# Zeroed dummy products in the planned gaps of TensorE, in a talking-heads attention and squared-ReLU kernel

## The chip, the cores and the metric

The kernel runs on one core of one Trainium2 chip. The metric is the device time of one execution in microseconds (us); lower is better. The kernel before took 604.01, 604.84 and 604.93 us in three runs, a median of 604.84 us.

## What is computed

The reference, cut to what matters (8 batches, 12 heads, 448 rows, head size 64; 3584 rows of 768 in the feed-forward part, hidden size 2048):

```python
scores = (1 / sqrt(64)) * q @ k.T                      # per batch and head, 448 x 448
scores = einsum('bhij,hg->bgij', scores, w_pre)        # heads are mixed
attn = softmax(scores, axis=-1)
attn = einsum('bhij,hg->bgij', attn, w_post)           # heads are mixed again
x = (attn @ v) as rows of 768
out = square(relu(x @ w_in)) @ w_out
```

## The kernel before

**Stages.** A batch has four blocks of score rows: a tail block (r = 0) and three blocks of 128 rows (r = 1 to 3). `score` makes the scores of a block per pair of heads on TensorE (L465 for the tail, L470 for the pairs), and VectorE or ScalarE copies them from a PSUM bank to the tile `snat`, of which there are two (`copy`, L300 and L302). `relayout` (the transfers L498, issued by SyncE) moves them to `sch`, so that ten query rows with all twelve heads lie on 120 partitions: a chunk. A batch has 45 chunks. `chunk` takes each through these steps: `f_m`, a product with `wmix` that mixes the heads (L563); `f_max`, the row's extreme on VectorE (L568); `f_exp`, the exponential and its sum on ScalarE (L571); `f_rc`, the reciprocal on VectorE (L577); `f_wq`, the second mixing matrix scaled by it on GpSimd (L580); `f_at`, four products that mix and turn at once (L587); and `f_ac`, a copy to `atb`. When half of a batch's rows are there, `av` multiplies by `v` (L623, 48 products for one half) and ScalarE copies the result to `xt`. The feed-forward part works on units of 128 or 256 rows: L668 (hidden layer), ScalarE's ReLU (L681), GpSimd's square (L684), L700 (output), a VectorE copy, a store.

**The start.** Batch 0 and 1 turn q and k by TensorE (L353, for the tail rows L381); later batches by DMA. GpSimd issues the loads of q, k and v, and in batch 0 those of both weight matrices of the feed-forward part (L775 issues `w_in`); each of the weight loads is placed behind an `f_wq`.

**What sets the order.** Nothing of it is left to the scheduler of the framework. Every step is an `Op` with a planned duration, a priority, what it depends on, and the PSUM bank that it takes or gives back. `Planner.run` goes through the time of a plan: whenever an engine is free in the plan it takes the ready step with the lowest priority number, and the order in which the steps were taken is the order in which the kernel then issues them (`manual_schedule`). The planned durations are constants in the code (190 ns for `f_m`, 212 ns for `f_at`); the chip doesn't see them, only the order. Each engine runs its instructions strictly in the order issued, and each waits for what it needs. The eight PSUM banks are given out by the planner from the front of the list `free`. TensorE's steps have a mode (whole array, half of its rows, half of its columns), and the planner puts 95 ns on a change of mode (`TURN`). The products of the feed-forward part have priorities above 1e6 and so fill what attention leaves free; there is none before the first half of batch 0 is through `av`.

## Time and profile before

| what | value |
|---|---|
| median of three runs | 604.84 us |
| profiled execution, whole | 606.62 us |
| its span, first to last instruction | 604.8 us |
| TensorE (PE) busy | 571.2 us, 94% |
| VectorE (DVE) busy | 489.7 us, 81% |
| ScalarE (ACT) busy | 468.4 us, 77% |
| GpSimd (POOL) busy | 325.6 us, 54% |
| granted TensorE clock, mean | 0.968 |

The profile is of one execution. Its parts that are used below: the span cut in 40 slices of about 15 us, in which each digit is the busy share in tenths and PEclk is the clock that TensorE was granted, in tenths of full speed; the chain of work that ended last, followed back from the last instruction, with the time at which each piece began and its length; windows, with the busy time of each engine in a stretch (in brackets the number of instructions), the granted clock, the busy share of the DMA engines and the GB/s; the timeline of one engine, where square brackets give the idle time before a piece and what ended it. A line L465 is line 465 of the kernel before. The ends of matmuls are modelled in the profile, so that small gaps on PE are shown smaller than they are.

### The profile page before, as it was taken

To read this page: it belongs to the slowest core of one execution; us is meant where nothing else is said; L and a number is where in the kernel's file an instruction comes from. 1 tells how busy PE (TensorE), PEld (TensorE's weight loads), DVE (VectorE), ACT (ScalarE), POOL (GpSimd) and SP (SyncE) were. 2 spreads that over 40 slices of the span, in tenths; PEclk is the share of its full clock that TensorE was granted. 3 is DMA by queue.
4 is the path that set the end of the run, shared out by engine and by line. 5 is a ranking of instruction groups with operands and counts; after the bars stand their busy time and mean duration, and the time that the engine had idled before them with its cause. 6 is when DMAs were issued, how large, how long until landed. Compare 5 with 4: busy or idle time off the path is not lost.

```text
span 604.8 us, 16567 instructions
## 1 busy us (share of the span) xinstructions
PE 571.2 (94%) x5517; PEld 405.6 (67%) x5517; DVE 489.7 (81%) x1237; ACT 468.4 (77%) x1223; POOL 325.6 (54%) x595
## 2 busy tenths in 40 slices
PE   4678889999999999999999999999999999999996
PEld 2335646666767857675867867686777867687873
DVE  4777987879898998989799998999899989887011
ACT  2677888878889898898898878899888887985320
POOL 5353816733665727662774727672783644472530
PEclk9757999979999999999999999999999999999999
DMA  9799989974498539974597439964797426321011
GB/s 135 119 227 168 205 158 162 191 135 111 116 150 199 147 82 169 196 148 115 123 169 178 129 91 187 170 151 114 149 190 152 131 83 144 97 92 29 27 53 52
DMA packets 138222, 82.29 MB, mean 136 GB/s; under 512 B 59672, under 2 KB 134680, under 8 KB 138136
## 3 DMA queue, kind: packets, MB, share of 16 engines
q1 hardware_dynamic: 86744, 58.42, 37.9%
q0 software_dynamic: 51392, 22.81, 30.6%
q8 instruction: 43, 0.70, 0.5%
q14 instruction: 43, 0.35, 0.2%
HBM read 45.62 MB, written 11.01 MB: 94 GB/s over the span
## 4 chain that ended last, share of the span: by engine, by line
PE 86%; DVE 5%; DMA 5%; issue 2%; POOL 2%; ACT 1%; DVEq 0%; POOLq 0%; ACTq 0%
PE bank L700 24%; PE bank L668 23%; PE bank L587 13%; PE bank L563 11%; PE bank L623 7%; PE bank L470 6%; DMA sch<-snat 4%; PE bank L465 2%; DVE mn L568 2%; DVE snat L300 1%; DVE atb L300 1%; POOL wq L580 1%; DMA qt<-in_q_dram 1%; PE bank L353 0%; POOL w L775 0%
## 5 line engine op out<-in xcount | busy, mean ns | idle before, releaser
L571 ACT ACTIVATE es<-bank,mn 120x448 bf16<-120x448 f32 x360 | 229.5, 644 | 33.8 <-DVE mn L568 27.2
L580 POOL TENSOR_SCALAR wq<-wback,rc 120x120 bf16<-120x120 f32 x360 | 130.8, 367 | 211.9 <-DVE rc L577 128.9
L568 DVE TENSOR_REDUCE mn<-bank 120x1 f32<-120x448 f32 x360 | 211.0, 611 | 5.9 <-PE bank L563 5.1
L700 PE MATMUL bank<-w,h 128*128 128x384 bf16 x896 | 174.5, 326 | 0.1
L300 DVE CAST atb<-bank 112x480 bf16<-112x480 f32 (+3 forms) x235 | 142.9, 619 | 36.5 <-PE bank L587 33.4
L668 PE MATMUL bank<-xt,w 128*128 128x256 bf16 (+1 forms) x1536 | 163.8, 259 | 0.0
L587 PEld LDWEIGHTS <-es 120*112 120x112 bf16 (+1 forms) x1440 | 120.8, 134 | 46.2 <-issue 20.7
L668 PEld LDWEIGHTS <-w 128*128 128x128 bf16 x1536 | 133.2, 98 | 25.2 <-issue 5.0
L587 PE MATMUL bank<-wq,es 120*112 120x120 bf16 (+1 forms) x1440 | 132.2, 222 | 14.1 <-POOL wq L580 12.6
L684 POOL TENSOR_TENSOR h<-hr 128x512 bf16<-128x512 f32 x112 | 116.5, 1041 | 48.5 <-ACT hr L681 46.6
L700 PEld LDWEIGHTS <-h 128*128 128x128 bf16 x896 | 83.0, 97 | 55.3 <-issue 6.7
L563 PE MATMUL bank<-sch,wmix 120*128 120x448 bf16 x352 | 115.1, 365 | 3.6 <-DMA sch<-snat 3.1
L302 ACT CAST snat<-bank 128x448 bf16<-128x448 f32 x174 | 88.0, 540 | 19.3 <-PE bank L470 10.5
L300 DVE CAST snat<-bank 128x448 bf16<-128x448 f32 x162 | 96.1, 614 | 2.7 <-PE bank L470 1.8
L681 ACT ACTIVATE hr<-bank 128x512 f32<-128x512 f32 x112 | 67.1, 599 | 34.2 <-PE bank L668 29.0
L302 ACT CAST atb<-bank 112x480 bf16<-112x480 f32 (+2 forms) x149 | 78.7, 537 | 19.0 <-PE bank L587 17.6
L571 ACT ACTIVATION_READ_ACCUMULATOR es<-bank,mn 120x1 f32 x360 | 75.7, 210 | 0.0
L577 DVE RECIPROCAL rc<-sm 120x1 f32<-120x1 f32 x360 | 53.5, 154 | 18.6 <-ACT es L571 16.5
L715 DVE COPY osb<-bank 128x384 f32<-128x384 f32 x56 | 30.9, 552 | 39.5 <-PE bank L700 39.5
L470 PE MATMUL bank<-kt,qz 64*128 64x448 bf16 x288 | 50.9, 372 | 2.1 <-DVE qz L300 1.8
L563 PEld LDWEIGHTS <-wmix 120*128 120x128 bf16 x360 | 32.4, 99 | 21.3 <-issue 9.2
L623 PE MATMUL bank<-atb,vs 112*64 112x192 bf16 (+1 forms) x768 | 43.8, 275 | 0.0
(45 smaller groups left out, 228.0 us busy)
## 6 DMA issues: line engine op xcount, KB each, us to landing
sch<-snat SPq DMA_DIRECT2D x336, 105.0 KB
out_dram<-osb SPq DMA_DIRECT2D x23, 360.0 KB
vs<-in_v_dram POOLq DMA_DIRECT2D x16, 336.0 KB, 8.7
ks<-in_k_dram POOLq DMA_DIRECT2D x14, 336.0 KB, 9.0
qs<-in_q_dram POOLq DMA_DIRECT2D x14, 288.0 KB, 8.7
w<-in_moe_w_in_dram POOLq DMA_DIRECT2D x6, 512.0 KB, 20.0
w<-in_moe_w_out_dram POOLq DMA_DIRECT2D x4, 768.0 KB, 17.5
out_dram<-osb SPq DMA_DIRECT2D x8, 192.0 KB
```

The lines of the kernel that those rows point to most:

```text
L300: nc.vector.tensor_copy(out=out_, in_=in_)
L302: nc.scalar.copy(out=out_, in_=in_)
L470: nc.tensor.matmul(slot[:, 0:S], lhsT=qz[i][half, r - 1, at_, :], rhs=kt[i][half, :, at_, :], start=True, stop=True,)
L563: nc.tensor.matmul(slot[:, 0:S], lhsT=wm[0:rows, :], rhs=src[0:rows, :], start=True, stop=True,)
L568: nc.vector.tensor_reduce(out=mn[i][0:rows, :], in_=slots[mk][0:rows, 0:S], axis=AX.X, op=ALU.min)
L571: nc.scalar.activation(out=es[i][0:rows, 0:S], in_=slots[mk][0:rows, 0:S], func=ACT.Exp, scale=-1.0, bias=mn[i][0:rows, 0:1], accum_out=sm ...
L580: nc.gpsimd.tensor_scalar(out=wq[i][0:rows, :, 0:ns], in0=wback[0:rows, :, 0:ns], scalar1=rc[i][0:rows, 0:1], scalar2=1.0, op0=ALU.mult, o ...
L587: nc.tensor.matmul(slot[0:P_KEYS, jb * H * ns:(jb + 1) * H * ns], lhsT=es[i][0:rows, jb * P_KEYS:(jb + 1) * P_KEYS], rhs=wq[i][0:rows, :, ...
L623: nc.tensor.matmul(v_[64 * hh:64 * hh + 64, i, 0:nx], lhsT=vs[:, 2 * c2 + hh, jb, :], rhs=atb[half][:, jb, 2 * c2 + hh, :], start=(jb == 0 ...
L668: nc.tensor.matmul(slot[:, j * w:(j + 1) * w], lhsT=w1[c2][:, (f0 + j) * 128:(f0 + j + 1) * 128], rhs=xt[:, c2, a:z], start=(c2 == 0), sto ...
L684: nc.gpsimd.tensor_tensor(out=h2_[:, f0:f0 + nf, 0:w], in0=hr[gi % 2][:, :].rearrange("p (f c) -> p f c", f=nf), in1=hr[gi % 2][:, :].rear ...
L700: nc.tensor.matmul(slot[:, 0:384], lhsT=h2_[:, ft, mt * 128:(mt + 1) * 128], rhs=w2[:, ft, nt * 384:(nt + 1) * 384], start=(ft == 0), stop ...
```

## The change

A tile `still` of 128 x 256 zeros (bfloat16) is set by VectorE as its first instruction. `stand` is one matmul on it, 256 columns wide, into a PSUM bank that nobody owns at that moment; its result is never read. The planner issues one whenever TensorE is free in the plan, has no ready step, and a bank is free, up to 190000 ns of the plan; it counts 112 ns for it (224 ns before 6000 ns of the plan), in which TensorE takes nothing else. It uses the mode of the step before. Twelve more are issued ahead of everything else. Since planned steps now begin a little later where a dummy was put ahead of them, the order of the other steps changes as well.

```diff
+IDLE_NS, IDLE_COLS, IDLE_END = 112, 256, 190000
+IDLE_COLD, COLD_END = 224, 6000
...
+                if item is None and eng == "PE" and free and self.still and t < IDLE_END:
+                    op = Op({"PE": 0}, 0, 0, self.still, [], None, None, mode)
+                    op.eng, op.ns, op.at = "PE", IDLE_COLD if t < COLD_END else IDLE_NS, t
+                    order.append((op, [free[0], mode]))
+                    busy[eng] = t + op.ns
+                    heapq.heappush(events, (t + op.ns, n, None))
+                    n += 1
...
+    still = sb.tile([P, IDLE_COLS], BF16, name="still")
+    nc.vector.memset(still[:, :], 0.0)
...
+    def stand(slot, mode):
+        k_, m_ = P // 2 if mode == ROWS else P, P // 2 if mode == COLS else P
+        nc.tensor.matmul(
+            slot[0:m_, 0:IDLE_COLS], lhsT=still[0:k_, 0:m_], rhs=still[0:k_, :], start=True, stop=True,
+        )
+
+    pl.still = stand
...
+        for _ in range(12):
+            stand(banks[0], 0)
```

In the built program there are 382 of them, in 88 groups, where TensorE had 5517 matmuls before: 28 ahead of the first transpose (L381), 87 more up to the first `f_m`, 156 from there to the `f_at` behind the first `av`, 80 from there to chunk 59, 27 among the chunks 60 to 65 and 4 later. In every group the last dummy writes the bank that the next product takes; 62 of the 382 wait for the copy that frees it.

More of the change, by code (lines that the diff above doesn't have):

```diff
@@ L80, in __init__ @@
         self.banks, self.most = [], {}
+        self.still = None
     def add(self, eng, ns, pri, fn, deps=(), lat=60, bank=None, frees=None, mode=0):
@@ L185, in run @@
                         push(x)
-        assert len(order) == len(self.ops)
+        assert len(order) >= len(self.ops)
         return order
```

## The prediction, as it was put on record

> **What bounds the kernel now.** I read the slices first, then the chain of waits, then windows cut where the clock changes, then the timelines of PE and SP.

> ```profile
> PE   4678889999999999999999999999999999999996
> ...
> PEclk9757999979999999999999999999999999999999
> ```

> PE is at 9 tenths from the seventh slice (91 us) on: from there the end is PE's work, done without a gap. What is lost lies before, in idle time and in a clock of 5 to 7 tenths in slices 2 to 4 and 9. The windows give the edges.

> ```profile
> 23.40:47.30 23.90, 18.31 (x97) 9.37 (x96) 17.72 (x44) 16.79 (x47) 12.72 (x24) 0.50 1.25 199
> 50.70:57.50 6.80, 6.44 (x63) 5.16 (x63) 3.80 (x11) 5.17 (x16) 3.07 (x6) 0.50 1.02 164
> 57.50:88.00 30.50, 23.98 (x323) 17.55 (x323) 28.42 (x75) 26.20 (x71) 15.21 (x30) 1.00 1.11 186
> 88.00:116.00 28.00, 27.32 (x266) 19.68 (x264) 22.33 (x54) 22.80 (x59) 19.08 (x32) 1.00 0.96 170
> 116.00:122.40 6.40, 5.48 (x40) 2.66 (x39) 6.14 (x18) 6.13 (x17) 4.15 (x10) 1.00 0.73 197
> 122.40:129.20 6.80, 6.32 (x63) 5.37 (x63) 3.54 (x10) 4.73 (x12) 2.46 (x5) 0.50 0.70 129
> ```

> The first figure is the length, the second PE's busy time, the third from the end the clock. It is half in 23.4 to 47.3, 50.7 to 57.5 and 122.4 to 129.2 us. The start is half too, though no record says so: two products L465 take 0.91 us at 11.55 and 0.66 us at 13.49 (chain).

> But a slow PE costs only where the end waits for it. The chain in those stretches:

> ```profile
> 26.53 8.52 DMA sch<-snat
> ...
> 37.04 8.87 DMA sch<-snat
> ...
> 53.33 3.98 PE bank L623 x37
> ```

> ```profile
> 122.88 0.56 PE bank L587 x4
> 123.44 3.98 PE bank L623 x24
> 127.42 0.98 PE bank L587 x8
> 128.40 1.02 PE bank L563 x3
> ```

> From 26 to 46 us the chain is two relayout transfers of 8.5 and 8.9 us. The waits in the program's order name eight DMA counters in turn for them, so a ninth transfer waits for the first: the one of 26.53 landed at 35.05, and SP issued the eighth after it at 35.12. A faster PE does nothing there. From 51 to 57.8 and from 122.9 to 129.4 the chain is PE at half clock.

> **The change part by part.** *One dummy* is a product of 256 columns. The trace has that form: 12 of L668 in 1.31 us (chain, at 110.76), so 0.109 us at full clock and 0.22 at half. Its weight load lies beside the product before, as L668's do. The 382 take 41.6 us of PE at full clock. Each one placed where PE would wait anyway costs nothing; every other one costs 0.109 us.

> *The first 28*: the zeros are VectorE's first instruction, and VectorE begins at 0.90 us. 28 at half clock take 6.1 us and end near 7.2 us. PE's first real work begins at 7.84 us, when the tail of q lands: hidden. If that cover were short by a microsecond it would cost that microsecond.

> *The 87 up to the first `f_m`*: 9.5 us. Here the loads are early, and PE does not wait as the plan thinks:

> ```profile
> 7.84 0.80 PE L381 MATMUL bank<-ident,qt 128*128 128x128 bf16 x6 [7.84 <-DMA qt<-in_q_dram]
> 8.57 0.96 PE L353 MATMUL bank<-ident,ks 112*64 112x112 bf16 x16
> 9.64 0.90 PE L465 MATMUL bank<-kt,zt 128*128 128x448 bf16 x2
> ...
> 17.00 0.62 PE L470 MATMUL bank<-kt,qz 64*128 64x448 bf16 x4 [0.79 <-DVE qz L300]
> ```

> No wait stands before the transposes L353, while the changed order puts 13, 10, 10 and 11 dummies ahead of groups of them. PE's own work from 7.84 to 18.01 us is 8.6 us, of which 5.2 at half clock would be 2.6: 6.0 us. With 9.5 us of dummies the first `f_m` comes at 23.3 us, not 18.01: **5 us later**. What passes on is what the relayouts see. The first waits for the tails (49 of the 87 ahead of the last): 7.84 + 5.3 + 3.4 = 16.5 against 14.15 us, +2.4. The first of the next block waits for the last pairs (90 ahead, 9.8 us): +5, less 0.7 us in which SP was behind at that place (copies done at 20.68, issue at 21.37): about +4. Since the transfers are then held by their own eight places up to 49 us, this stays: +2.4 to +4.3; I take **+3.7**, near the latter, the one that the stream of eight begins with.

> *The 156 up to 57.8 us*: 17.0 us of dummies. PE's records in 18.0 to 57.5 us are 2.69 + 18.31 + 1.98 + 6.44 us busy; at full clock 2.69 + 9.16 + 1.98 + 3.22 = 17.0. Together 34 us in a stretch of 39.5: they fit, nearly without slack, so they cost nothing there as long as the clock is full. The gain: PE in the chain from 51.06 to 57.78 is 6.7 us (0.52, 0.49, 0.86, 0.40, 3.98, 0.47) at half clock; at full it is 3.35. So **-3.4**, and batch 0's `av` ends at +0.3.

> *The 80 up to 116 us*: 8.7 us, where PE's idle time is 6.5 + 0.7 = 7.2 us (first minus second figure of two windows above); gaps are shown too small, since the ends of matmuls are modelled. **+0.5**, between 0 and 1.5.

> *The 27 up to 122.4 us*: 2.9 us against 0.9 us idle by the records, but the chain from 116.9 to 122.8 us is VectorE and GpSimd, so that most of it is hidden: **+0.5**, between 0 and 2.0. They fill the gaps after which the clock falls. If it stays, the four pieces of chain above (6.54 us at half) take 3.27: **-3.3**.

> *Waits*: 62 dummies wait for the copy that frees their bank. In all 88 groups the next product takes the same bank and would wait for it. Nothing.

> *After 130 us* no dummy stands, but the order differs. PE is busy 59.92 of 60 us in 130 to 190; another order moves a dense stretch by changes of mode and small waits: between -1 and +1 us, taken as 0. The zeroing on VectorE (0.38 us for the larger one at 0.90 us) lies in idle time.

> Sum: +3.7 - 3.4 + 0.5 + 0.5 - 3.3 = -2.0 us. Against the profiled execution (span 604.8, whole 606.62 us) this is 604.6; the median of the runs, 604.84, stands 1.8 under that execution, so **602.8 us**.

> [...] In 118.9 to 122.4 us PE was busy 2.86 of 3.50 us, its longest wait was below 0.8 us, and yet the clock then halved; in 30.1 to 33.6 PE was dense and the clock did not rise. So busy time alone does not decide: 2.28 of 3.50 us busy at 71.1 to 74.6 kept the clock. [...]

> **The rivals.**
> 1. *The dummies are real work, slower.* The 107 behind 57.8 us take 11.7 us where the records show 8.1 idle. If the head's delay goes through whole (+5 - 3.4 = +1.6), PE then has no waits to fill, and the excess of 3.6 us is paid; with -3.3 for the clock at 122: 606.7 us. It decides from the point where PE waits less than 11.7 us between 57.8 and 122 us. For it: DVE is busy 28.42 of 30.50 us in 57.5 to 88, so PE's waits there belong to VectorE and are not lengthened; against it: the records show gaps too small.
> 2. *The clock at 122 falls all the same*, since gaps below a microsecond are not its cause: the sum without -3.3 is +1.3, 606.1 us, at the edge of 0.2%. For it: the kept clock at 71 us with more idle time; against it: no stretch at 95% or more lost the clock.
> 3. *Zeros don't count for the clock at all.* Then the dummies cost 0.22 us: 34 + 17 us in 18 to 57.5, some 12 us late, 616 us or more. For it: no row shows a product of zeros. Against it: nothing in the clock's edges follows data.
> 4. *The relayouts go faster*, since the first weight load comes later behind the first `f_wq` and the early transfers escape it: the head passes on 2.4 us or less, 601 us. I count it to the forecast.

> **How the numbers follow.** Forecast with 4: 0.57, of it 0.50 faster by over 0.2% and 0.07 within 0.2%; rival 1: 0.22, slower; rival 2: 0.16, of it 0.08 within 0.2%, 0.08 slower; rival 3: 0.05, slower. 0.2% is 1.2 us, about what a measurement of this kernel can tell from no change. So faster 0.50, same 0.15, slower 0.35. The forecast's own range is 600.5 to 604.9: its ends are -4.3 (head +2.4, both +0.5 at 0) and +0.1 (head +4.3, one +0.5 at 2.0). The reordering moves the lower end to 600.0, taken at half its size. For 8 in 10 the range reaches over rivals 1 and 2: 600.0 to 607.0.

> **What would show it.** Right: PEclk full from about 8 us to 130 us; the first `f_m` at 22 to 24 us; `av` (L623) of batch 0 taking 2 us, ending near 57.5 us; L623 at 122 us taking 2 us. Wrong: a first `f_m` near 18 us (the dummies at the head are hidden); dummies of 0.2 us; the relayout transfers no longer in the chain; or, in 58 to 122 us, PE dense and each chunk later than before.

## The result: slower by 0.28%, and the profile after

The changed kernel takes 606.64 us in the median of 9 runs, the kernel before 604.93 us in the median of 9 beside it: ratio 1.0028, 95% interval 1.0017 to 1.0038. One of the nine executions of the changed kernel took 674.77 us at a mean granted clock of 0.85; the ratio leaves it out. The forecast was 602.8 us; the sign was wrong. The profiled execution after has a span of 605.6 us, against 604.8. In every run of both kernels the time lies 1.8 us over the span. So the execution that I had before me (606.62 us) was itself 1.7 us longer than the kernel's median, which matters below.

The clock did what the change sets out to do. The slices of the page, after:

```profile
PE   8999899999999999999999999999999999999996
...
PEclk9999999999999999999999999999999999999999
```

And the windows that were shown of before (length, PE busy, then PEld, DVE, ACT, POOL, the clock, DMA share, GB/s):

```profile
23.40:47.30 23.90, 23.33 (x222) 16.74 (x218) 20.51 (x51) 17.59 (x47) 13.00 (x24) 1.00 1.02 169
50.70:57.50 6.80, 6.80 (x94) 5.17 (x95) 6.34 (x18) 6.49 (x19) 2.72 (x7) 1.00 1.01 177
57.50:88.00 30.50, 27.53 (x372) 21.16 (x366) 25.47 (x67) 24.93 (x67) 15.37 (x29) 1.00 1.14 185
88.00:116.00 28.00, 28.00 (x273) 20.12 (x271) 23.00 (x57) 21.90 (x58) 17.29 (x30) 1.00 0.97 167
116.00:122.40 6.40, 6.40 (x64) 4.80 (x62) 6.14 (x17) 5.79 (x16) 5.38 (x11) 1.00 0.76 221
122.40:129.20 6.80, 6.80 (x67) 4.53 (x67) 6.80 (x19) 6.39 (x20) 3.08 (x7) 1.00 0.79 148
```

The clock is whole from 6.3 to 603.6 us, and PE is never idle for long. Yet a busy PE is not a gain when what fills it is dummies. PE's timeline after (L861 is the dummy, L365 the transposes, L680 the hidden layer of the feed-forward part, L599 `f_at`):

```profile
8.41 1.58 PE L861 MATMUL bank<-still 128*128 128x256 bf16 x13
9.92 0.58 PE L365 MATMUL bank<-ident,ks 112*64 112x112 bf16 x16
...
11.48 1.25 PE L861 MATMUL bank<-still 128*128 128x256 bf16 x10
12.66 0.58 PE L365 MATMUL bank<-ident,ks 112*64 112x112 bf16 x16
```

```profile
63.97 1.24 PE L680 MATMUL bank<-xt,w 128*128 128x128 bf16 x19 [1.63 <-DMA w<-in_moe_w_in_dram]
73.01 0.37 PE L599 MATMUL bank<-wq,es 120*112 120x120 bf16 x4 [1.03 <-POOL wq L592]
```

A group of 16 transposes takes 0.58 us in place of 0.96, but 13 dummies of 0.109 us stand ahead of one group and 10 ahead of the next, where PE did not wait before. Later PE waits 1.63 us for the last piece of `w_in`, a wait that was not there before. It comes with the new order, as the experiments show: that order without any dummy has it too (1.31 us). Where the time went, from the starts of the same steps in both traces (us):

| step | before | after | difference |
|---|---|---|---|
| first `f_m` | 18.01 | 23.66 | +5.65 |
| first `av` of batch 0 begins | 53.26 | 55.60 | +2.34 |
| its last product ends | 57.31 | 57.77 | +0.46 |
| second `av` of batch 0 begins | 91.38 | 94.83 | +3.45 |
| first `av` of batch 1 begins | 123.37 | 128.73 | +5.36 |
| its last product ends | 127.42 | 130.90 | +3.48 |
| last `av` begins | 557.2 | 559.9 | +2.7 |

The steps stand in another order, so that the difference at one step is no difference in the work done; at the end it is the spans' 0.8 us.

### The profile page after: what moved, and what is told of

Same layout as the page of the kernel before. It is cut to its first block, busy times and chain, and to the rows that moved or that the text cites. A ratio compares the mean times of both kernels' runs of the same rounds, so it can differ in the third digit from the quotient of the medians.

```text
span 605.6 us, 17331 instructions
## 1 busy us (share of the span) xinstructions
PE 594.1 (98%) x5899; PEld 429.8 (71%) x5899; DVE 487.7 (81%) x1240; ACT 475.2 (78%) x1232; POOL 321.2 (53%) x584
## 4 chain that ended last, share of the span: by engine, by line
PE 91%; DMA 5%; POOL 2%; issue 1%; DVE 0%; ACT 0%; DVEq 0%; POOLq 0%; ACTq 0%
PE bank L680 24%; PE bank L712 24%; PE bank L599 13%; PE bank L575 11%; PE bank L635 6%; PE bank L482 6%; DMA w<-in_moe_w_in_dram 4%; PE bank L861 4%; PE bank L477 2%; PE bank L365 1%; DMA qt<-in_q_dram 1%; POOL wq L592 1%; POOL w L787 0%; POOL qt L255 0%; POOL ks L260 0%
## 5 line engine op out<-in xcount | busy, mean ns | idle before, releaser
L312 DVE CAST atb<-bank 112x480 bf16<-112x480 f32 (+2 forms) x226 | 136.2, 616 | 37.7 <-PE bank L599 34.5
L680 PE MATMUL bank<-xt,w 128*128 128x256 bf16 (+1 forms) x1536 | 163.7, 259 | 1.6 <-DMA w<-in_moe_w_in_dram 1.6
L680 PEld LDWEIGHTS <-w 128*128 128x128 bf16 x1536 | 132.8, 98 | 26.3 <-issue 5.5
L599 PEld LDWEIGHTS <-es 120*112 120x112 bf16 (+1 forms) x1440 | 115.4, 130 | 29.2 <-issue 8.4
L599 PE MATMUL bank<-wq,es 120*112 120x120 bf16 (+1 forms) x1440 | 126.8, 217 | 1.4 <-POOL wq L592 1.3
L575 PE MATMUL bank<-sch,wmix 120*128 120x448 bf16 x352 | 111.9, 354 | 0.6 <-DVE atb L312 0.6
L314 ACT CAST atb<-bank 112x480 bf16<-112x480 f32 (+2 forms) x158 | 83.5, 538 | 14.7 <-PE bank L599 13.0
L861 PE MATMUL bank<-still 128*128 128x256 bf16 (+1 forms) x382 | 58.7, 281 | 1.4 <-DVE still L266 1.1
L482 PE MATMUL bank<-kt,qz 64*128 64x448 bf16 x288 | 48.3, 357 | 0.0
L861 PEld LDWEIGHTS <-still 128*128 128x128 bf16 (+1 forms) x382 | 37.0, 100 | 11.8 <-DVE still L266 1.1
```

The lines of the kernel that those rows point to most:

```text
L312: nc.vector.tensor_copy(out=out_, in_=in_)
L314: nc.scalar.copy(out=out_, in_=in_)
L482: nc.tensor.matmul(slot[:, 0:S], lhsT=qz[i][half, r - 1, at_, :], rhs=kt[i][half, :, at_, :], start=True, stop=True,)
L575: nc.tensor.matmul(slot[:, 0:S], lhsT=wm[0:rows, :], rhs=src[0:rows, :], start=True, stop=True,)
L599: nc.tensor.matmul(slot[0:P_KEYS, jb * H * ns:(jb + 1) * H * ns], lhsT=es[i][0:rows, jb * P_KEYS:(jb + 1) * P_KEYS], rhs=wq[i][0:rows, :, ...
L680: nc.tensor.matmul(slot[:, j * w:(j + 1) * w], lhsT=w1[c2][:, (f0 + j) * 128:(f0 + j + 1) * 128], rhs=xt[:, c2, a:z], start=(c2 == 0), sto ...
```

## The experiments

In the kernels a, b and d the planner and so the order of all other steps are those of the changed kernel (b4 moves two loads), and only the issue of the dummies differs, by the time that the plan gives them; the kernels c keep the order of the kernel before. For a2_no_head the edit reads

```diff
+KEEP = ((0, 3500), (21900, 200000))
...
         for op, args in pl.run():
+            if op.fn is stand and not any(a <= op.at < z for a, z in KEEP):
+                continue
             op.fn(*args)
```

Main theory at the start: the head's dummies cost the time, by way of the late last load of `w_in`, and the order is neutral. Rivals: the order costs; or the 107 dummies behind 57.8 us do. Each ratio is to runs of the kernel before on the same chip (medians 604.82 to 605.16 us). The executions of one row spread over 1 to 7 us, so that a difference of about 1 us between two rows is not told from none.

| label | dummies issued | median us | ratio, 95% interval |
|---|---|---|---|
| a1_none | none | 602.56 | 0.9963, 0.9945 to 0.9981 |
| b7_open_28 | 28 opening | 600.78 | 0.9936, 0.9911 to 0.9960 |
| d3_156 | 28 + 156 | 600.72 | 0.9933, 0.9917 to 0.9950 |
| d2_156_half | 28 + 156 of half width | 601.84 | 0.9951, 0.9933 to 0.9969 |
| a2_no_head | 28 + 267 | 602.03 | 0.9950, 0.9934 to 0.9967 |
| b3_no_head_no_80 | 28 + 156 + 31 | 602.47 | 0.9948, 0.9928 to 0.9968 |
| a4_only_27 | 27 | 602.88 | 0.9947, 0.9928 to 0.9967 |
| d1_head_half | 28 + 87 of half width | 603.51 | 0.9984, 0.9963 to 1.0004 |
| b6_head_only | 28 + 87 | 607.85 | 1.0039, 1.0021 to 1.0057 |
| a3_no_80 | all but 80 | 607.40 | 1.0033, 1.0018 to 1.0048 |
| b4_w_in_early | all, two loads moved | 606.52 | 1.0020, 1.0004 to 1.0035 |
| c3_before_open_28 | before's order, 28 | 603.40 | 0.9982, 0.9970 to 0.9993 |
| c4_before_27 | before's order, 27 | 605.43 | 1.0005, 0.9995 to 1.0015 |

**The order alone** (KEEP empty, and not the first 12).

> The changed kernel's own order of all other steps, but none of the 382 dummies is issued. It gives the price of the new order alone. Main theory (the new order is about neutral; the loss comes from the dummies at the head, which delay the last load of w_in, and nothing of that is won back later): within 1 us of the kernel before, 604 to 606 us, clock again half in about 24 to 57 and near 122 us. Rival theory (the dummies are innocent, the new order costs): 606 us or more, as the changed kernel.

602.56 us. Neither theory had this: the new order is 2.6 us *faster* (by the interval of the ratio, 1.1 to 3.3 us). So the dummies, as they are executed, cost 4.1 us (606.64 - 602.56).

**Without the head's 87** (the diff above).

> As the changed kernel, its order kept, without the 87 dummies between the first transpose and the first f_m; the 28 opening ones and the 267 later ones stay. Main theory (head's delay, late w_in): first f_m near 18 us, the last w_in load issued near 34 us and landed before PE asks for it, no wait of 1.6 us near 64 us; 601 to 603.5 us. Rival theory (the 107 dummies behind 57.8 us are work that PE has no room for, wherever the head ends): the head was already paid back at 57.8 us, so 605.5 to 606.6 us.

602.03 us, 4.6 less than the changed kernel: the head's dummies cost the time, and the rival with the later 107 falls. That the last load of `w_in` is the way is not shown by this.

**Without the 80** (KEEP from 0 to 55800 and from 114600 on).

> As the changed kernel, its order kept, without the 80 dummies between the end of batch 0's first av and chunk 59; the head's 87 stay. Main theory: the wait for w_in near 64 us stays (1.6 us), later gaps win back under 1.5 us: 605 to 606 us. Rival theory (these dummies are the excess work): 2.5 us or more are won, 602.5 to 604 us.

607.40 us, above both expected ranges: nothing won. They were not the excess work.

**The head alone** (KEEP from 0 to 21900), **and the opening alone** (KEEP from 0 to 3500).

> The changed kernel's order with the 28 opening dummies and the head's 87 alone; none behind the first f_m. Main theory (the head's delay of some 5.5 us passes through to the end, the later dummies cost and win about nothing together): 4 to 5 us above the order without dummies (602.56), 606 to 607.5 us. Rival (the delay is absorbed where nothing holds PE to the plan's pace, since later gaps are open again): under 604.5 us.

> The changed kernel's order with the 28 opening dummies alone, which run before the first data are there. Main theory: the clock is full from 5 to 8 us on, the transposes at the head take half their time, the first f_m comes 1.5 us earlier than in the order without dummies; 0.5 to 1.5 us of that remain: 601 to 602 us. Rival (the head waits for loads, not for PE): 602.5 us, no difference.

607.85 and 600.78 us: the 87 dummies of the head cost 7.1 us when nothing else differs. The opening ones gain 1.8, though the intervals of b7 and a1 overlap. SP's relayout transfers in the two traces show how it passes on; the first column is the start, the last the number. The opening alone:

```profile
13.46 4.91 SPq L511 DMA_DIRECT2D sch<-snat  x6
...
19.16 13.41 SPq L511 DMA_DIRECT2D sch<-snat  x14
...
34.53 28.10 SPq L511 DMA_DIRECT2D sch<-snat  x25
```

With the head's 87:

```profile
17.44 4.92 SPq L511 DMA_DIRECT2D sch<-snat  x6
...
23.14 15.37 SPq L511 DMA_DIRECT2D sch<-snat  x14
...
40.67 21.24 SPq L511 DMA_DIRECT2D sch<-snat  x19
```

The stream of relayouts starts 4.0 us later and is 6.1 us later at 35 to 41 us. The first `av` begins at 50.53 against 56.57 us, the last at 552.8 against 560.1. Nothing is caught up. The last load of `w_in` is issued later by as much, at 39.39 against 33.09 us, and PE waits for it 1.5 us with the head's dummies and 1.7 us without.

**The head at half width** (KEEP from 0 to 21900).

```diff
-            op.fn(*args)
+            op.fn(*args, **({'n': 128} if op.fn is stand and op.at >= 3500 else {}))
```

> 28 opening dummies and the head's 87, the latter 128 columns wide instead of 256, in the changed kernel's order. If the head's loss is the time that PE spends in them (5 to 7 us for 9.5 us of dummies), half the width gives about half the loss: 603.5 to 604.8 us, first f_m near 20 us. If the loss comes from their number or from waits, 606 us or more.

603.51 us: 2.7 us over the opening alone, where full width costs 7.1. The first `f_m` comes at 19.35 us, 2.5 us later than with the opening alone; at full width it is 6.4 us later. The loss follows the time that PE spends in them, not their number. The executions of this kernel spread from 600.22 to 607.27 us, so that the 2.7 is a rough figure.

**The 156, at full and half width** (KEEP from 0 to 3500 and 21900 to 55800; half width as above).

> 28 opening dummies and the 156 between the first f_m and the first av, 256 columns wide, no others, in the changed kernel's order. The clock stays full to 55 us, where it is half from 22 to 50 us with the opening ones alone (600.78). If full clock in that stretch is worth what PE saves in the chain, 597.5 to 599.5 us; if the dummies take back what the clock gives, 600.5 to 602.5 us.

> The same as d3_156 with the 156 at 128 columns. If they hold the clock at half the price, up to 1.5 us less than d3_156; if the clock falls again, as with the opening ones alone or some tenths above, 600.8 to 601.5 us.

600.72 and 601.84 us, against 600.78 without the 156; the first lies where it was expected if the dummies take back what the clock gives. The clock is the difference between the two traces in 23.4 to 47.3 us. The opening alone, and then with the 156:

```profile
23.40:47.30 23.90, 19.08 (x96) 9.15 (x95) 19.29 (x48) 16.51 (x45) 11.52 (x23) 0.50 1.22 202
```

```profile
23.40:47.30 23.90, 21.72 (x204) 15.33 (x203) 19.37 (x49) 17.14 (x48) 11.65 (x23) 1.00 1.25 206
```

VectorE and the DMA engines do the same in both (19.29 and 19.37 us busy, 202 and 206 GB/s), and the first `av` begins at 50.53 and 50.72 us. Full clock in this stretch, without a head's delay, is worth nothing that can be measured. Transfers end last there; the chain of the opening alone has, from 23 to 58 us,

```profile
23.49 8.25 DMA sch<-snat
...
33.09 25.13 DMA w<-in_moe_w_in_dram
```

and the chain with the 156 has the same load of `w_in`:

```profile
33.07 25.11 DMA w<-in_moe_w_in_dram
```

So PE waits at the same place until the same time, with the opening alone and then with the 156 (L681 is the hidden layer):

```profile
58.26 1.24 PE L681 MATMUL bank<-xt,w 128*128 128x128 bf16 x19 [1.72 <-DMA w<-in_moe_w_in_dram]
```

```profile
58.23 1.79 PE L681 MATMUL bank<-xt,w 128*128 128x128 bf16 x19 [1.51 <-DMA w<-in_moe_w_in_dram]
```

What a faster PE wins ahead of 58 us ends in this wait. The order without any dummy waits there too (1.31 us, until 60.78 us). Half width holds the clock as well (whole from 4.0 to 58.6 us) and brings no more; its interval covers the others. That the 156 take back what the clock gives is all the same unlikely: at half that price nothing more is left.

This holds for the stretch, not for the clock as such. Of the eight executions of the opening alone, the five with a mean granted clock of 0.975 to 0.980 took 600.18 to 601.15 us, the three with 0.968 to 0.972 took 602.60 to 602.84. A lower clock goes with 2 us there; where in those three it fell, and whether it is the cause, no trace shows.

**Without the head's 87 and the 80** (KEEP 0 to 3500, 21900 to 55800, 114600 on).

> The changed kernel's order with 28 + 156 + 31 dummies: without the head's 87 and without the 80 between 57.8 and 116 us. If those 80 are neutral, 602 us as with only the head's taken out; if they hold PE back (gaps in which it would catch up are filled), 1 us or more less, 601 us.

602.47 us, not less than 602.03: the 80 are neutral, within the spread.

**The load of `w_in` sooner** (all dummies; the fifth and sixth load moved in the issued order).

```diff
+        late = [steps[i] for i in w1_at[4:]]
+        steps = [x for i, x in enumerate(steps) if i not in w1_at[4:]]
+        steps[w1_at[3] + 1:w1_at[3] + 1] = late
```

> The changed kernel with all its dummies; only the last two loads of w_in are issued by GpSimd right behind the fourth, some 6 us earlier, all other orders kept. Main theory (part of the head's cost is the late last load, for which PE waits 1.6 us near 64 us): the wait is gone and 1 to 2 us are won, 604.6 to 605.6 us. Rival (the wait only takes the place of others behind it): 606 to 607 us.

606.52 us, as the rival said. The wait of 1.6 us is gone from the trace, and with it 0.9 us of the span, but the median is that of the changed kernel. The edit did less than it was meant to. The chains of the changed kernel and then of this run have

```profile
39.73 24.20 DMA w<-in_moe_w_in_dram
```

```profile
32.91 30.13 DMA w<-in_moe_w_in_dram
```

The last load is issued 6.8 us sooner and lands only 0.9 us sooner, and the chain still goes through it. So the wait as such is not the loss (the opening alone has one of 1.7 us), but whether the head's delay is passed on by the load of `w_in` or by the relayouts stays open.

**The clock at 122 us** (KEEP 114600 to 122500; the kernel before twice, unchanged; and before's order with 27 dummies put in by hand, c4).

```diff
+        for n in range(60, 66):
+            extra[at_op[n]] = 4
+        for n in (65, 66, 68):
+            extra[m_op[n]] = 1
         for op, args in pl.run():
+            for _ in range(extra.get(op, 0)):
+                stand(args[0], 0)
             op.fn(*args)
```

> The changed kernel's order with only the 27 dummies among the chunks 60 to 65. If small gaps there are what lowers the clock at 122 us, the clock stays full in 119 to 130 us while it is half as before in 24 to 57 us, and the time is 2.5 to 3.3 us under that of the order without any dummy. [...]

> The kernel before once more, for a second profile: the one that the prediction was made from took 606.62 us, 1.7 us above the median of its runs, with the clock half for 37.5 us. If the fall of the clock at 122 us is in every execution, it is here too, and the time is 604 to 606.6 us; if it is in some, and costs 2 to 3 us, a profile without it shows 603.5 to 604.5 us.

> The same as the run above, a third profile, with the same two cases.

> The kernel before in its own order, with 27 dummies put ahead of the six f_at of chunks 60 to 65 (four each) and three f_m there, and no others. If gaps there lower the clock at 122 us and that costs 3 us: clock full in 119 to 130 us, about 34 us of half clock left of 37, 602.5 to 603.5 us. If the half clock there costs little in a usual execution, or comes all the same: 604.5 to 605.5 us.

a4 gave 602.88 us, no less than without any dummy (602.56), and c4 605.43, no less than before. a4 tests little, since in the trace without dummies the clock does not fall there either. In c4 the clock stays whole at 122 us, but the 27 dummies themselves take 2.9 us of PE; whether a gain of that size is taken back by them or isn't there, the run does not tell apart. The kernel before, executed again, took 605.69 and 604.35 us. In c1 the clock was half up to 57.3 us (its first record is the rise there; until 51 us a single `f_m` takes 0.53 to 0.58 us, against 0.36 at full clock) and in 88.0 to 91.4, and it did not fall at 122:

```profile
116.00:122.40 6.40, 5.84 (x49) 3.33 (x46) 6.14 (x15) 6.13 (x16) 4.54 (x9) 1.00 0.59 201
122.40:129.20 6.80, 5.82 (x81) 4.29 (x80) 5.44 (x17) 6.17 (x18) 3.30 (x8) 1.00 0.65 126
```

In c2 it was half for 3.4 us there. So the fall comes in two of three executions of the kernel before, and the length that I had priced, 6.8 us, in one. For `av` alone it costs what I said where it comes: it takes 4.05 us in the profile before and 2.17 in c1 and in the changed kernel. But the 27 dummies that were to prevent it are not hidden: all of them stand in the chain after, between 120.39 and 125.36 us, with 2.85 us together, for instance

```profile
122.04 0.54 PE bank L861 x5
...
122.93 0.66 PE bank L861 x6
```

**The opening in before's order** (the planner untouched).

```diff
+        for _ in range(28):
+            stand(banks[0], 0)
         for op, args in pl.run():
             op.fn(*args)
```

> The kernel before in its own order, with 28 dummies ahead of everything and no other. If the gain of the opening dummies (1.8 us in the changed kernel's order) comes from the full clock at the head, it is 1 to 2 us here too: 603 to 604 us. If it belonged to the other order, 605 us.

603.40 us, 1.6 less than before (by the interval of the ratio, 0.4 to 1.8 us): the gain of the opening belongs to the head's clock, not to the order.

**The best version** of all is the changed kernel's order with the opening dummies alone, 600.78 us, 0.64% under the kernel before (0.40 to 0.89%); the 156 may stand or go.

## Why the prediction was wrong, point by point

- *Price of a dummy*: right. 13 took 1.42 us of the chain after, 0.109 each.
- *The first 28 are hidden*: right in cost (they ran from 1.06 to 6.8 us, PE's first work began at 8.07). What they bring, the full clock at the head, I had counted within the head's own sum (5.2 us at half clock taken as 2.6). Alone it is worth 1.6 to 1.8 us.
- *The head*, "5 us later" at the first `f_m`, of which "+3.7" passes on: this is the effect of the 28 and the 87 together. Against the kernel before the first `f_m` is 5.65 us later, as forecast. In the new order, with nothing else changed, it is 4.9 us later (18.38 us with no dummy, 23.30 with the opening and the head) and 5.3 us reach the end (607.85 against 602.56). Right in kind and 1.6 us too small: nothing is caught up, so that what the first `f_m` loses reaches the end whole.
- *The gain in the first stretch*, "-3.4": **this is the step that failed.** It took PE's share of the chain in 51 to 58 us at half clock as something that the 156 dummies would halve, and so put PE's clock at the end of a stretch in which transfers end last. In the new order the 156 gain nothing (600.72 against 600.78): PE waits for the last piece of `w_in` until 58.23 us with them and 58.26 without. Nor is the half clock in 51 to 58 us there without them: the clock rises by itself at 49.9 us with the opening alone, at 51.2 with no dummy at all, both ahead of `av`, and at 46.8 in one of the repeated executions of the kernel before (c2). Behind the head's dummies, the 156 and the 31 last ones together bring 0.5 us (607.85 to 607.40). What the 156 would do in the order of the kernel before was not run.
- *The end of the first `av`*: the forecast +0.3 against +0.46 measured is luck. In the traces the new order alone moves it by -1.7 us, the opening and the head by +3.1, all later dummies by -1.0. Even the first of these is not more than what one execution of the kernel before differs from another: there it ends at 57.31, 58.12 and 55.1 us.
- *The 80, "+0.5"*: neutral by themselves (b3, a3). The 3 us that the trace loses between 57.8 and 94.8 us come with the head: with the 87 and no later dummy (b6) the second `av` begins at 95.83 us, with all later ones and without the 87 (a2) at 88.93, with the opening alone at 88.87.
- *The 27 and the clock at 122 us*, "+0.5" and "-3.3": the 27 were to be hidden for the most part, and stand in the chain after with 2.85 us, which leaves 0.4 us of the 3.3. And the fall of the clock is shorter or absent in other executions of the kernel before. I read a price from one execution that was 1.7 us longer than the median and took it off the median.
- *After 130 us*, the new order "between -1 and +1 us, taken as 0": -2.6 us for the whole order (interval of the ratio 0.9945 to 0.9981). Part of it is won ahead of 130 us: in 122 to 130 us PE is busy for all 8.00 us at full clock in the order without dummies, in the kernel before for 6.99 at full clock (c1) or 8.00 at a clock of 0.79 (c2). Which of the moved steps does it was not settled.
- *The signs* named for a right forecast all came: the clock, the first `f_m` at 23.66 us, `av` of batch 0 in 2.17 us ending at 57.77, the next one in 2.17 us. So did one named for a wrong forecast: PE dense in 58 to 122 us and the chunks later. They show that the clock did what was meant, and not what it is worth.
- *Rival 1* gave 606.7 and the measured time is 606.64, which is luck too: that the head's delay goes through whole holds, but it is 5.3 us and not 5 less 3.4, and that the 107 are excess work doesn't hold (a2). *Rival 2*: its premise was not told apart, since the clock stayed up at 122 us both with 27 dummies (c4) and without (c1). *Rival 3* fell: zeros hold the clock (whole from 4.1 to 58.7 us with the 156, half from 22.6 to 49.9 without them). *Rival 4* did not come: with the head 14 relayouts are issued over 15.37 us, against 13.41 with the opening alone.

In medians the steps from kernel to kernel are: order -2.6, opening -1.8, the 87 of the head +7.1, all later ones behind such a head -1.2 (607.85 to 606.64). They add up to +1.5 by construction, against +1.7 measured beside the kernel before; the second and the last are near the spread of the runs. The forecast had 0 for the order, +3.7 for the opening and the head (here +5.3) and -5.7 for all later ones (here -1.2): most of the miss lies in the last.

## What to carry to other kernels

A filler is free only where the engine waits on the chip, not where a plan says so: PE ran the dummies in the order issued, and where data came sooner than planned, they stood ahead of ready work (the 13 at 8.57 us, for 1.42 us, ahead of transposes that had not waited before). Before a higher clock is given a price, ask which wait ends last in that stage, and ask it of the changed kernel's order too; from 23 to 58 us transfers did, and the clock's worth was nil there. Ahead of the first data, where the filler was free, it gained 1.6 to 1.8 us. And one profile is one execution: a stretch whose clock differs between executions should be priced from several, and the order that a planner makes should be run alone, since it can move more than the edit itself.
